# The prologue of an attention and MLP kernel: three query groups on the first keys, one token tile's statistics on ScalarE

## The chip, the cores and the metric

The kernel runs on one core of a Trainium2 chip. The core has five engines that run side by side, each with its own in-order queue: TensorE (PE, matrix products into PSUM; its weight loads are shown as PEld), VectorE (DVE), ScalarE (ACT), GpSimd (POOL) and SyncE (SP), which here only issues transfers between the main memory and the on-chip buffer SBUF. The metric is the time of one execution on the device, in microseconds. The kernel before takes 1042.89 us, the median of three runs from 1042.58 to 1043.29.

## The reference

```python
def _A_ref(x, wqkv, wo):            # S = 2048 tokens, D = 1024, H = 32 heads of 32
    qkv = (x @ wqkv).reshape(B, S, 3, H, Dh).transpose(2, 0, 3, 1, 4)
    q, k, v = qkv[0], qkv[1], qkv[2]
    p = softmax(einsum("bhqd,bhkd->bhqk", q, k) * Dh ** -0.5)
    o = einsum("bhqk,bhkd->bhqd", p, v)
    return o.transpose(0, 2, 1, 3).reshape(B, S, D) @ wo

def _B_ref(x, w1, b1, w2, b2):      # F = 3584
    h = gelu(layernorm(x) @ w1 + b1)     # tanh form
    return h @ w2 + b2

xn = layernorm(x)
out = x + _A_ref(xn, wqkv, wo) * silu(_B_ref(xn, w1, b1, w2, b2))
```

Everything is in bfloat16. The softmax takes no maximum off: the kernel raises the scaled scores directly.

## The kernel before, in words

**Tiles.** The 2048 tokens are 16 tiles of 128, and 8 blocks of 256. The 32 heads are 8 groups of 4 heads; a head group `hg` fills 128 rows. A *query group* is 256 queries of one head group, so there are 64 of them. A *unit* (`unit`, from L800) is one query group against one block of 256 keys: eight matmuls of scores into four PSUM banks (L811), two exponentials of 128x1024 on ScalarE (L820), which write a buffer of probabilities `P`, and later eight matmuls of the probabilities with the values. 512 units make 1024 exponentials. Six of the eight PSUM banks hold scores, so TensorE can be one and a half units ahead of ScalarE. The other two banks serve all other products, one item of work in each.

**Denominators.** For most query groups VectorE adds the probabilities pairwise into one tile (`tree`: four pair adds and three adds per query group) and TensorE sums this tile with a matrix of ones. In the first query groups, TensorE sums every unit's probabilities directly (`plain`). `quotient` divides.

**The prologue.** Ten token tiles are loaded at once into what later is the MLP's hidden buffer `hT` (`load_x`, L616); tiles 10 to 15 follow as buffers come free. Each tile gets two `bn_stats` of 512 columns and one `bn_aggr` on VectorE (L761, L763), an addition of epsilon (L767), a power of -0.5 on GpSimd (L769), and a normalization on VectorE (`normalize`, L738). Tiles 0 and 1 are groups of their own here, the others go in pairs. Tiles 0 to 3 are transposed by TensorE (`tr_item`, L725) and copied out of PSUM by ScalarE (L728); tiles 4 to 15 are transposed by a DMA that SP issues (L742). The result is `xnT`. For every block of 256 tokens, `k_item` computes the keys of head group 0 (copied to SBUF by ScalarE, L714), `q_item` or `qk_item` the queries (copied by VectorE, L704 and L694), and `v_item` the values (L682). While the keys come, only two query groups of head group 0 use them: the list `order0` (L1088) is (0,0), (0,1), (1,0), (1,1), and then for each further block (0,kp), (1,kp), each pair being a query group and a key block.

**Buffers.** There are ten buffers for probabilities, used in turn. The first 16 units also use six more that lie in the weight rings `w1r` and `w2r` of the MLP, which are not loaded until these have been read.

**After the prologue.** The units of the remaining query groups follow one another through all head groups. Between them TensorE does the projections of the next head group, the MLP (whose tanh also runs on ScalarE, L1004 and L1033), and at the end the output projection.

**The order of the work.** All queues are written by a planner (`_Plan`) before the kernel is built. Every operation has an assumed duration, a latency, a priority and the operations that it depends on, found by tokens such as `("xnT", t)` that it reads and writes. The planner plays the engines against the clock with these assumptions: at each moment an engine takes the ready operation of lowest priority number (`pick`). `plan.dense` holds the queues of TensorE's items, each item with a position, and some with a unit by which it is due. Scores go first as soon as their PSUM banks are free. Where TensorE has nothing to do, the planner puts in filler matmuls (L660). On the chip the order is then fixed, and only semaphores hold an engine up.

## Time and profile before

| what | us |
|---|---|
| median of three runs (lowest, highest) | 1042.89 (1042.58, 1043.29) |
| span of the profiled execution | 1042.1 |
| ScalarE busy | 1017.7 (98%) |
| TensorE busy, its weight loads | 1008.8 (97%), 640.8 (61%) |
| VectorE busy | 958.4 (92%) |
| first tile's statistics start on VectorE | 3.61 |
| first copy of a transposed tile on ScalarE | 8.79 |
| first exponential | 13.63 |
| key copies of blocks 0 to 7 on ScalarE | 12.74, 18.54, 25.09, 29.61, 34.23, 40.45, 44.07, 47.95 |
| last exponential ends | 1031.5 |

The profile is one execution; of that execution only the span from the first to the last instruction is known, and the runs' times, taken around the whole execution, are 0.5 to 1.2 us longer. In the lines that follow, a line of a timeline has the start, the length, the engine, the source line, the operation with output and input, and how many were merged; in brackets stands the idle time before it and what ended it. Lengths of merged rows overlap by a little, so the step from one instruction to the next is better taken from their starts. A line of waits has the waiting engine and line, what it waited for, the total, the number and the longest.

### The profile page before, as it was taken

What the parts mean: (1) busy time and instruction counts of PE and PEld (TensorE: products, weight loads), DVE (VectorE), ACT (ScalarE), POOL (GpSimd) and SP (SyncE); (2) the same over time, 40 slices, a digit from 0 to 9 for tenths busy, and PEclk for the clock granted to TensorE, in tenths of its full rate; (3) what the DMA queues carried; (4) which work ended last, traced back from release to release, by engine and by line L of the source; (5) the groups of instructions that cost most, each with busy time, mean ns of one, the idle gap of its engine ahead of it and who ended that gap; (6) DMA issues with size and microseconds to landing.
All of it is one profiled execution on the core that took longest, in us unless ns stands there. A gap on an engine that the chain in (4) does not pass through costs nothing.

```text
span 1042.1 us, 31753 instructions
## 1 busy us (share of the span) xinstructions
PE 1008.8 (97%) x14179; PEld 640.8 (61%) x14179; DVE 958.4 (92%) x1450; ACT 1017.7 (98%) x1129; POOL 11.0 (1%) x20
## 2 busy tenths in 40 slices
PE   9999899999999999999999999999999999999996
PEld 7555567666665676667665765666657655754442
DVE  8589998999899999998999989999999999878887
ACT  5899999999999999999999999999999999999996
POOL 1200000000000000000000000000000000000000
PEclk9999999999999999999999999999999999999999
DMA  8985558537654577376555674575456753763321
GB/s 198 193 224 145 128 169 226 143 98 204 183 167 127 152 210 217 91 185 181 149 143 157 175 219 128 125 198 169 135 137 195 204 168 121 224 212 111 105 82 52
DMA packets 318200, 168.00 MB, mean 161 GB/s; under 512 B 56688, under 2 KB 306032, under 8 KB 318064
## 3 DMA queue, kind: packets, MB, share of 16 engines
q1 hardware_dynamic: 318064, 165.98, 58.3%
q8 instruction: 111, 1.82, 0.7%
q14 instruction: 25, 0.20, 0.1%
HBM read 146.55 MB, written 12.06 MB: 152 GB/s over the span
## 4 chain that ended last, share of the span: by engine, by line
ACT 89%; PE 4%; DVE 3%; DMA 3%; SPq 0%; issue 0%; POOL 0%
ACT P L820 82%; ACT ut L1004 5%; PE ps L610 3%; ACT gw L1033 2%; DVE stats L761 1%; PE ps L605 1%; PE ps L811 1%; DMA hT<-in_A_x_dram 1%; DMA w2r<-in_B_w_dram 1%; ACT w1r L820 1%; DMA yst<-in_A_x_dram 1%; ACT w2r L820 1%; DMA xnT<-gw 0%; DVE gw L738 0%; DMA yT<-yst 0%
## 5 line engine op out<-in xcount | busy, mean ns | idle before, releaser
L820 ACT ACTIVATE P<-ps 128x1024 bf16<-128x1024 f32 x1012 | 956.6, 1237 | 4.3 <-PE ps L811 4.2
L837 DVE TENSOR_TENSOR PA<-P 128x2048 bf16<-128x2048 bf16 x178 | 216.4, 1219 | 26.3 <-ACT P L820 25.6
L610 PE MATMUL ps<-yT,w1r 128*128 128x256 bf16 x1792 | 227.5, 273 | 1.0 <-DVE xb L992 0.4
L610 PE MATMUL ps<-w2r,hT 128*128 128x256 bf16 x1792 | 222.3, 273 | 0.4 <-DMA w2r<-in_B_w_dram 0.4
L811 PE MATMUL ps<-QKT 32*128 32x256 bf16 x4096 | 203.3, 273 | 18.4 <-ACT P L820 16.7
L854 DVE TENSOR_TENSOR PR<-PR,PA 128x2048 bf16<-128x2048 bf16 x178 | 216.2, 1214 | 1.3
L610 PEld LDWEIGHTS ps<-yT,w1r 128*128 128x128 bf16 x1792 | 163.8, 98 | 51.7 <-issue 27.9
L610 PEld LDWEIGHTS ps<-w2r,hT 128*128 128x128 bf16 x1792 | 163.9, 98 | 48.1 <-issue 29.1
L811 PEld LDWEIGHTS ps<-QKT 32*128 32x128 bf16 x4096 | 60.7, 92 | 152.8 <-ACT P L820 146.6
L605 PE MATMUL ps<-P,V 128*32 128x256 bf16 x4048 | 138.0, 274 | 0.0
L610 PE MATMUL ps<-xnT,wqk 128*128 128x512 bf16 (+1 forms) x552 | 130.4, 365 | 0.2 <-ACT xnT L728 0.2
L605 PEld LDWEIGHTS ps<-P,V 128*32 128x32 bf16 x4048 | 96.1, 96 | 30.6 <-issue 22.8
L610 PE MATMUL ps<-wv,xnT 128*128 128x256 bf16 (+1 forms) x576 | 87.2, 285 | 2.7 <-DVE V L682 1.4
L610 PEld LDWEIGHTS ps<-xnT,wqk 128*128 128x128 bf16 x552 | 48.4, 98 | 51.2 <-issue 13.7
L992 DVE TENSOR_TENSOR xb<-ps,b1T 128x512 bf16<-128x512 f32 x112 | 76.6, 684 | 1.4 <-PE ps L610 1.0
L837 DVE TENSOR_TENSOR PR<-P 128x2048 bf16<-128x2048 bf16 x62 | 75.4, 1215 | 1.4 <-ACT P L820 1.1
L1004 ACT ACTIVATE ut<-ut 128x1024 bf16<-128x1024 bf16 x56 | 70.9, 1266 | 0.0
L610 PEld LDWEIGHTS ps<-wv,xnT 128*128 128x128 bf16 x576 | 52.1, 98 | 27.4 <-issue 11.2
L694 DVE CAST QKT<-ps 128x512 bf16<-128x512 f32 x59 | 40.4, 685 | 2.8 <-PE ps L610 2.4
L1001 DVE TENSOR_TENSOR ut<-xb 128x1024 bf16<-128x1024 bf16 x56 | 38.3, 683 | 0.2
L1003 DVE TENSOR_TENSOR ut<-ut,xb 128x1024 bf16<-128x1024 bf16 x56 | 38.0, 679 | 0.0
L909 DVE STREAM_TRANSPOSE nt<-ps 128x256 f32<-128x256 f32 x64 | 28.4, 443 | 10.3 <-PE ps L605 10.2
(76 smaller groups left out, 564.9 us busy)
## 6 DMA issues: line engine op xcount, KB each, us to landing
w1r<-in_B_w_dram SPq DMA_DIRECT2D x112, 512.0 KB, 4.5
w2r<-in_B_w_dram SPq DMA_DIRECT2D x128, 448.0 KB, 4.4
hT<-in_A_x_dram SPq DMA_DIRECT2D x20, 256.0 KB, 4.0
wqk<-in_A_wqkv_dram SPq DMA_DIRECT2D x16, 256.0 KB, 3.8
yst<-in_A_x_dram SPq DMA_DIRECT2D x16, 256.0 KB, 4.6
g_scratch<-gw SPq DMA_DIRECT2D x32, 128.0 KB, 3.9
o_scratch<-ot SPq DMA_DIRECT2D x56, 64.0 KB, 3.6
xnT<-o_scratch SPq DMA_DIRECT2D x7, 512.0 KB, 5.7
```

What stands on the lines that cost most here:

```text
L605: ins = e.matmul(dst(j), lhsT=lhsT(j), rhs=rhs(j), start=start, stop=stop, tile_position=(0, 32 * j), skip_group_check=True)
L610: return e.matmul(dst, lhsT=lhsT, rhs=rhs, start=start, stop=stop, skip_group_check=True)
L694: dve(lambda e: e.tensor_copy(QKT[sl][:, which, tq * 512:(tq + 1) * 512], bank(it.bank)), c_ps(512), [], [(nm, sl, 2 * tq), (nm, sl, 2 * t ...
L811: ins = e.matmul(bank(b0[j], kk * 256, (kk + 1) * 256), lhsT=QKT[sl][32 * j:32 * j + 32, 1, kb * 128:(kb + 1) * 128], rhs=QKT[sl][32 * j:3 ...
L820: x = act(lambda e, h=h: e.activation(Pt[pi][:, 2 * h:2 * h + 2].rearrange("p j k q -> p (j k q)"), ps[:, pr[h] * 1024:(pr[h] + 1) * 1024] ...
L837: return dve(lambda e: e.tensor_tensor(dst[:].rearrange("p u j q -> p (u j) q"), src[:].rearrange("p u j k q -> p (u j) k q")[:, :, 0, :], ...
L854: return dve(lambda e: e.tensor_tensor(fl3(pr), fl3(pr), fl3(PA[i]), op=ALU.add), c_b16(2048), [("PA", i), tok], [tok], 3.2)
L909: dve(lambda e: e.transpose(nt_t[:], bank(pv.bank, 256, 512)), c_ps(256) + 120, [], [("nt",)], prio, pv)
L992: dve(lambda e: e.tensor_tensor(xb_t[ui][:, half].rearrange("p (k t) -> p k t", k=2), bank(it.bank).rearrange("p (k t) -> p k t", k=2), b1 ...
L1001: dve(lambda e: e.tensor_tensor(u_, fl(xb_t[ui]), fl(xb_t[ui]), op=ALU.mult), c_b16(1024), xs, [("ut", ui)], 3)
L1003: dve(lambda e: e.tensor_tensor(u_, u_, fl(xb_t[ui]), op=ALU.mult), c_b16(1024), [("ut", ui)] + xs, [("ut", ui)], 3)
L1004: act(lambda e: e.activation(u_, u_, ACT.Tanh, scale=GC), c_acts(1024), [("ut", ui)], [("ut", ui)], 1)
```

## The change

Five things change, all of them in how the first 60 us are arranged; the computation is the same.

1. Three query groups instead of two (`NG0 = 3`) take part while the keys come. `order0` puts the units (2,0) and (2,1) behind block 2, (2,2) behind block 5, (2,3) behind block 6, and (2,4) to (2,7) behind the last of the first two groups. The queries of block 2 and block 3 become `q_item`s of 256 columns. The first four units of group 2 get buffers of their own (16 to 19): in the values' third slot, in the next head group's queries and in two pieces of the hidden buffer. Group 2 gets its denominators from TensorE.
2. Tile 1 (`AT = 1`) gets its mean and its mean of squares from two activations on ScalarE with an accumulator, and three small operations on VectorE turn them into the variance.
3. Tile 1's copy out of PSUM is made in two halves, and `xnT` is tracked by column block, so that a product can begin with the first half.
4. Tiles 2 and 3 become groups of their own; their loads go ahead of the first weights; the wait of tile 2's statistics for tile 1's normalization goes.
5. In the planner, VectorE's aggregates and epsilon additions go ahead of statistics, and in the first 16 us VectorE is held for up to 0.13 or 0.22 us when a more urgent operation is about to become ready.

```diff
+            if e == "DVE" and best is not None and 1 <= best.prio <= 1.2 and t < 16000.0:
+                for r, _, o in soon[e]:
+                    if r < t + (220.0 if o.prio > 0.96 else 130.0) and o.prio < best.prio - 0.04 and not o.dead:
+                        wake(r, e)
+                        return None
...
-        NTR, NWARM = 4, 8
+        NTR, NWARM, NG0, AT = 4, 8, 3, 1
...
+        Pt.append(V[:, 2].rearrange("p t n -> p (t n)").rearrange("p (j k q) -> p j k q", j=4, k=2))
+        Pt.append(QKT[1][:, 0].rearrange("p (j k q) -> p j k q", j=4, k=2))
         h_flat = hT[:].rearrange("p a b c -> p (a b c)")
+        for i in range(2):
+            Pt.append(h_flat[:, (3 + i) * 2048:(4 + i) * 2048].rearrange("p (j k q) -> p j k q", j=4, k=2))
...
-        load_x(0)
-        load_x(1)
+        for t in range(NTR):
+            load_x(t)
         wk0 = load_qk(0, 1)
         wq0 = load_qk(0, 0)
-        load_x(2)
-        load_x(3)
...
-            act(lambda e: e.activation(xnT[:, :, t * 128:(t + 1) * 128],
-                                       bankb(it.bank).rearrange("p (c t) -> p c t", c=DC), ACT.Copy),
-                c_act(1024), [tk], [("xnT", t)], 0, it)
+            for lo, hi in ((0, 4), (4, 8)) if t == 1 else ((0, 8),):
+                act(lambda e, lo=lo, hi=hi: e.activation(xnT[:, lo:hi, t * 128:(t + 1) * 128],
+                                                         bankb(it.bank)[:, lo * 128:hi * 128].rearrange("p (c t) -> p c t", t=128),
+                                                         ACT.Copy),
+                    c_act((hi - lo) * 128), [tk], [("xnT", t, c) for c in range(lo, hi)], 0, it)
...
-            groups = [(2 * n,), (2 * n + 1,)] if n == 0 else [(2 * n, 2 * n + 1)]
+            groups = [(2 * n,), (2 * n + 1,)] if n < 2 else [(2 * n, 2 * n + 1)]
             for ts in groups:
+                if ts == (AT,):
+                    for k, f, sc in ((0, ACT.Copy, 1.0 / D), (1, ACT.Square, D ** -0.5)):
+                        act(lambda e, k=k, f=f, sc=sc: e.activation(
+                            fl3(PA[0])[:, k * 1024:(k + 1) * 1024], xst[AT], f, scale=sc, accum_out=mv[:, AT, k:k + 1]),
+                            c_acts(1024) + 93, [XS(AT)], [("st", AT, k)], 1)
+                    dve(lambda e: e.tensor_tensor(lnp[:, AT:AT + 1, 2], mv[:, AT:AT + 1, 0], mv[:, AT:AT + 1, 0], op=ALU.mult), 65,
+                        [("st", AT, 0)], [("s2",)], 0.95)
+                    dve(lambda e: e.scalar_tensor_tensor(lnp[:, AT:AT + 1, 0], mv[:, AT:AT + 1, 1], EPS, lnp[:, AT:AT + 1, 2], op0=ALU.add,
+                                                         op1=ALU.subtract), 65,
+                        [("st", AT, 1), ("s2",)], [("ve", AT)], 0.95)
+                    dve(lambda e: e.tensor_tensor(mv[:, AT:AT + 1, 1], mv[:, AT:AT + 1, 1], lnp[:, AT:AT + 1, 2], op=ALU.subtract), 65,
+                        [("st", AT, 1), ("s2",)], [("mv", AT)], 1.1)
...
-                            605, [XS(t)], [("st", t, c)], 1.2, extra=[first[1]] if t == 2 else [])
+                            605, [XS(t)], [("st", t, c)], 1.2)
...
-                pro_q.append(q_item(n))
+            if n < NG0:
+                pro_q.append(q_item(n))
...
-                q0_q.append(qk_item(0, 0, n // 2, wq0, (0.5, 14.0, 28.0)[n // 2 - 1]))
-                q0_q[-1].due = 16 * (n // 2)
+                if n == 3:
+                    q0_q.append(q_item(3, "q0", 6.0))
+                else:
+                    q0_q.append(qk_item(0, 0, n // 2, wq0, (0.5, 14.0, 28.0)[n // 2 - 1]))
+                q0_q[-1].due = 16 * (n // 2) + (8 if n == 3 else 0)
...
-        pvs = [_Item("pv"), _Item("pv")]
-        us = [[], []]
-        order0 = [(0, 0), (0, 1), (1, 0), (1, 1)] + [(qb, kp) for kp in range(2, NKP) for qb in range(2)]
+        pvs = [_Item("pv") for _ in range(NG0)]
+        order0 = [(0, 0), (0, 1), (1, 0), (1, 1), (0, 2), (1, 2), (2, 0), (2, 1)]
+        for kp in range(3, NKP):
+            order0 += [(0, kp), (1, kp)]
+            if kp in (5, 6):
+                order0.append((2, kp - 3))
...
-        for qb in range(2):
+        for qb in range(NG0):
+            if qb == 2:
+                for kp in range(4, NKP):
+                    got[(2, kp)] = unit(0, 2, kp, pvs[2])
...
-                if w == 0 and qb < 2:
+                if w == 0 and qb < NG0:
```

More of the change, by code (lines that the diff above doesn't have):

```diff
@@ L691, in fn @@
                     return mm(e, bank(b), wqk[wi][:, dc, :], xnT[:, dc, tq * 512:(tq + 1) * 512], dc == 0, dc == DC - 1)
[L692 removed]
+                chunk(it, fn, Q512, [("xnT", 4 * tq + k, dc) for k in range(4)] + [("wqk", wi)])
             nm = "Q" if which == 0 else "K"
@@ L1103, in bass_recurrent_scan__mha_block__mixer_channel_mlp__prompt_kernel @@
             store_o(qb)
+        after([("V", 2, n) for n in range(NPR)], [("P", 16, h) for h in range(2)])
+        after([("Q", 1, n) for n in range(NPR)], [("P", 17, h) for h in range(2)])
+        after([("h", k) for k in range(12, NH)], [("P", i, h) for i in (18, 19) for h in range(2)])
         for i in range(3):
```

50 lines of the change are left out of this document (30 added, 20 removed).

## The prediction

> **What bounds the kernel now.** I read three things in this order: the first part of the page with the chain that ended last, ScalarE's own timeline of the first 60 us, and the waits and idle work of TensorE.
>
> ```profile
> span 1042.1 us, 31753 instructions
> ## 1 busy us (share of the span) xinstructions
> PE 1008.8 (97%) x14179; PEld 640.8 (61%) x14179; DVE 958.4 (92%) x1450; ACT 1017.7 (98%) x1129; POOL 11.0 (1%) x20
> ```
>
> ScalarE is busy 98% of the span, and the chain that ended last gives it 89%, of which 82% is one line, the exponentials of the scores. Merged in the chain, 100 of them take 91.67 us, so the step from one to the next is 0.917 us; the 1237 ns mean of the groups overlaps and is not used. From 47 us to 1031.5 us ScalarE has no idle slice worth a number (0.26 us in all, between 600 and 700 us). So the end is the moment at which ScalarE becomes saturated, plus a fixed amount of work. Time can only come from its idle time in the prologue:
>
> ```profile
> 19.43 5.63 ACT L820 ACTIVATE P<-ps 128x1024 bf16<-128x1024 f32 x6 [0.51 <-PE ps L811]
> 25.09 0.38 ACT L714 ACTIVATE QKT<-ps 128x256 bf16<-128x256 f32 x1
> 25.97 3.77 ACT L820 ACTIVATE P<-ps 128x1024 bf16<-128x1024 f32 x4 [0.50 <-PE ps L811]
> 29.61 0.42 ACT L714 ACTIVATE QKT<-ps 128x256 bf16<-128x256 f32 x1
> 31.50 2.86 ACT L820 ACTIVATE P<-ps 128x1024 bf16<-128x1024 f32 x3 [1.48 <-PE ps L811]
> 34.23 0.40 ACT L714 ACTIVATE QKT<-ps 128x256 bf16<-128x256 f32 x1
> 34.49 2.89 ACT L820 ACTIVATE P<-ps 128x1024 bf16<-128x1024 f32 x3
> 38.40 1.94 ACT L820 ACTIVATE P<-ps 128x1024 bf16<-128x1024 f32 x2 [1.01 <-PE ps L811]
> 40.45 0.38 ACT L714 ACTIVATE QKT<-ps 128x256 bf16<-128x256 f32 x1
> 41.34 2.85 ACT L820 ACTIVATE w1r<-ps 128x1024 bf16<-128x1024 f32 x3 [0.50 <-PE ps L811]
> ```
>
> The reader is to see a rhythm. Each L714 copies one block of 256 keys out of PSUM; these come every 3.6 to 6.6 us, while two query groups make only four exponentials (3.67 us) of each. Why the keys come at that pace is in the timeline of VectorE, which has no gap between 8.4 and 22.8 us:
>
> ```profile
> 14.80 0.65 DVE L761 BATCH_NORM_STATS2 stats<-hT 128x6 f32<-128x512 bf16 x1
> 15.36 0.16 DVE L767 TENSOR_SCALAR lnp<-mv 128x2 f32<-128x2 f32 x1
> 15.42 1.28 DVE L761 BATCH_NORM_STATS2 stats<-hT 128x6 f32<-128x512 bf16 x2
> 16.61 0.99 DVE L738 TENSOR_SCALAR gw<-hT,mv,lnp 128x1024 bf16<-128x1024 bf16 x2
> ```
>
> Here L738 normalizes tiles 4 and 5, the source of key block 2, and three statistics of tiles 6 and 7 stand before it.
>
> **The change, part by part.** Between the start of block 2's exponentials (25.97) and 47.05 lie 21.1 us. ScalarE does 18 exponentials in them (16.5) and 4 key copies at 0.28 from the chain (1.1), so 3.4 us are idle; the waits marked in the rows make 3.0 of it.
>
> 1. A third query group. After it, block 2 brings eight exponentials (7.3 us) and blocks 3 to 7 bring four or six, by the new list of units. With the old arrival times of the keys, ScalarE would finish block 2's eight at 33.3, when block 3 has been there since 29.6; the four of block 3 with its copy end at 37.3, block 4's at 41.2, and block 5's scores were there by 41.3. So one after another the 3.4 us fill: gain 3.4.
>
> 2. Block 2 sooner. On VectorE, tile 1 leaves: two statistics at a step of 0.62 (three start-to-end in 1.87) are 1.24 and an aggregate is 0.11; the wait of 0.35 for tile 2's load at 8.40 goes, as that load moves up. In come three small operations for tile 1 instead of one and a second addition of epsilon for tiles 2 and 3, about 0.08 each by the steps of L767: 0.25. Net 1.45. The new order (aggregates and epsilon ahead of statistics, and a short hold of VectorE) would also take statistics out from ahead of L738: at most the three above, 1.87; the one at 14.80 (0.56) and some 0.2 of the last are what it can surely free, because L738 must in any case wait 0.7 for GpSimd's power, which covers one statistic. I take 1.45 + 0.75 = 2.2. Lower end 0.5, if the holds (up to 0.22 each, some four before tile 5) take 0.95 back; upper end 1.45 + 1.87 = 3.3. What is late next is the pair of transposing loads of tiles 4 and 5 on SP (3.76 us for both from 17.18), then block 2's matmuls at 23.91; they follow L738 and move with it.
>
> 3. ScalarE gets tile 1's copy and square of 1024 columns: nearest row, the 1024-column copy out of PSUM, 1.03 us each, so 2.06. Tile 1 has landed by 4.85 at the latest (its first half is then in work), so they end by 6.9, inside the 6.6 us that ScalarE idles before 8.79. If that cover failed, the first exponential would be up to 2.1 later; that costs nothing either while the first eight exponentials wait for block 2. After a first exponential at about 12.3, eight of them, tiles 2 and 3's copies (1.87) and a key copy end at 21.8, and block 2's scores are due at 23.8: 2.0 us of cover.
>
> 4. Tile 1's copy in two halves: one more instruction, 0.07 us (from 0.28 for 256 columns and 0.93 for 1024), and the first matmuls may start half a copy, 0.45, sooner. Both lie within the same cover, so 0. The first keys come perhaps 1.3 us sooner, which moves nothing that ends last.
>
> 5. Loads: tiles 2 and 3 (512 KB) pass the first weights on SP. Data flowed at 235 to 275 GB/s while weights came and at 340 to 400 otherwise, by the bandwidth in slices of 0.3 us; the same six transfers end at about 7 to 8 us. The first use of the weights is at about 9.3. Cost 0; if they were 2 us late, part 3's cover takes it. The stalled issue (1.54 us for one) passes from tile 2 to tile 4, used after 10 us.
>
> 6. Group 2 now adds its denominators on TensorE (eight steps of 0.22, before one: +1.5 us), and VectorE loses seven adds of 1.21 (8.5 us). More sharply, TensorE must do the later work in 5 us less:
>
> ```profile
> PE ps L811 <- ACT P L820: 11.5, 21, 1.2
> ```
>
> ```profile
> 0.00:20.00 20.00, 11.13 (x141) 10.47 (x141) 1.00 0.79 192
> ...
> sum 1042.00, PE 21.93 PEld 18.88; mean PE 1.69 PEld 1.45
> ```
>
> The first row is TensorE's idle time before scores between 100 and 900 us; the second view is the filler matmuls, 21.93 - 11.13 = 10.8 us after 20 us. Some 22 us are spare, against 6.5 needed: 0. Without that cover the whole gain would go.
>
> By matmul busy time (97%) TensorE has 33 us left in the whole span. [...]
>
> 7. New waits. The queues are in order: at 28.84 VectorE waited 0.94 for tile 12's load with tile 11's aggregate behind it until 30.04. Such a misplaced wait can now cost ScalarE directly. Its bounds are 0 and 2.5 (the two largest old gaps, 1.48 and 1.01, again); block 5 is the tightest, due at 39.1 where ScalarE asks for it at 39.4. I take 0.7.
>
> Sum: 3.4 + 2.2 - 0.7 = 4.9 us off. The profiled span is 1042.1, and the median 1042.89 is 0.8 more; span 1037.2, time 1038.0. With the ends, 3.4 + 0.5 - 2.5 = 1.4 and 3.4 + 3.3 = 6.7, so 1036.2 to 1041.5.
>
> **Rivals.** (a) Keys stay as late: block 2 does not move (holds and loads eat part 2) and in-order waits take half of part 1 or more: 0 to 2 us off, 1040.9 to 1042.9. For it: tiles 10 to 15 wait for loads issued behind transposes on SP (28.84), which nothing here changes. Against: two tasks less ahead on VectorE.
>
> (b) Slower: the probability buffers. Unit (2,6) writes the buffer of (1,0), which group 1's product must have read. Before, that product started at about 55.5 after the last values (cast at 53.98) and the buffer was asked for at 56.6. Now ScalarE asks at about 58.9: twelve exponentials and two key copies after 41.2 in part 1 make 36 exponentials at 52.8, less 2.2, plus 0.7, is 51.3; eight more and a key copy are 7.6. In the meantime TensorE has three score units more ahead (1.3 us) and a third group's product close behind, 8 x 0.44 = 3.5 us. A delay of the values to 57 us would only eat the gain; it turns the sign when group 1's product starts more than 4.9 us after the request, near 64 us. With 7 to 9 us of such stall, 1045 to 1047. Against: TensorE is 96% busy from 50 to 60 and 98% from 60 to 80, but key, value and score work go ahead of the rest.
>
> (c) More: block 2 comes 3.3 sooner, nothing waits, and the head start of the first keys counts too (another 1.3): 8 us off, 1034.9.
>
> (d) The square makes ScalarE change its table. The trace has one load, 1.28 us at 0.72, for exponential, tanh and copy; it shows no square. Two more loads would put the first exponential 2.6 later, 0.6 beyond the cover: 1038.6. [...]
>
> **How the numbers follow.** The forecast 0.66 (its range 1036.2 to 1041.5), (a) 0.12, (b) 0.11, (c) 0.06, (d) 0.05. The measurement cannot tell less than 0.2%, 2.1 us, from no change, so faster means under 1040.8: most of the forecast (0.62 of 0.66), (c) and (d), 0.73; same is (a) and the rest of the forecast, 0.16; slower is (b), 0.11. The range runs from 1034.7, which takes in (c), to 1042.5, which leaves out (b) and a little of (a).
>
> **What would show it.** Block 2's key copy at 22.9 instead of 25.09, with eight exponentials behind it; ScalarE's idle time between the first exponential of block 2 and saturation under 1 us instead of 3.4; no statistic of tile 1 on VectorE; the first exponential near 12.3 instead of 13.63; 36 exponentials done near 51.3 us instead of 56.7; one table load. Wrong would be: a gap on ScalarE after 55 us (b), a wait of ScalarE for scores at blocks 4 to 6 of more than 2 us (a), or less idle time before 100 us with gaps between 600 and 700, where it was already 0.26.

## The result and the profile after

| what | before | after |
|---|---|---|
| median of 18 runs, us (lowest, highest) | 1043.09 (1041.59, 1044.37) | 1040.23 (1039.0, 1042.81) |
| ratio (95% interval) | 1 | 0.9972 (0.9965 to 0.9979) |
| span of the profiled execution | 1042.1 | 1039.2 |
| first exponential | 13.63 | 13.31 |
| block 2's first exponential | 25.97 | 22.41 |
| 41st exponential | 60.01 | 56.45 |
| key copies of blocks 2 to 7 | 25.09, 29.61, 34.23, 40.45, 44.07, 47.95 | 21.46, 28.76, 34.12, 38.71, 45.93, 48.95 |

The change takes 2.9 us off (0.28%), in the runs as in the two profiled executions; the forecast was 4.9. The result shows the span of every run: a run's time is 1.8 us more than its own span, not 0.5 to 1.2 us as the comparison of one span with other runs' times had it. So both profiled executions are some 0.8 us longer than their medians, and their spans can be compared.

The first lines of the page after, and its chain of work that ended last:

```profile
span 1039.2 us, 31689 instructions
PE 999.7 (96%) x14117; PEld 639.2 (62%) x14179; DVE 950.5 (91%) x1444; ACT 1020.1 (98%) x1134; POOL 11.7 (1%) x21
ACT 92%; PE 3%; DVE 3%; DMA 1%; issue 0%; POOL 0%
```

ScalarE bounds the kernel as before, and a little more of the chain is its own. Its timeline after, from the first work to the exponentials of block 6 (L771 are tile 1's statistics, L739 the copies of transposed tiles, L724 the key copies, L856 the exponentials):

```profile
0.72 1.28 ACT L655 ACT_TABLE_LOAD   x1 [0.72 <-PEq L1351]
4.14 1.06 ACT L771 ACTIVATE PA<-hT 128x1024 bf16<-128x1024 bf16 x1 [1.92 <-DMA hT<-in_A_x_dram]
5.10 0.19 ACT L771 ACTIVATION_READ_ACCUMULATOR PA<-hT 128x1 f32 x1
...
7.36 1.02 ACT L739 ACTIVATE xnT<-ps 128x1024 bf16<-128x1024 bf16 x1 [1.03 <-PE ps L735]
...
12.39 1.02 ACT L739 ACTIVATE xnT<-ps 128x1024 bf16<-128x1024 bf16 x1 [0.34 <-PE ps L735]
13.31 1.93 ACT L856 ACTIVATE P<-ps 128x1024 bf16<-128x1024 f32 x2
...
22.41 3.77 ACT L856 ACTIVATE P<-ps 128x1024 bf16<-128x1024 f32 x4 [0.50 <-PE ps L847]
...
35.98 2.85 ACT L856 ACTIVATE P<-ps 128x1024 bf16<-128x1024 f32 x3 [1.47 <-PE ps L847]
...
43.20 1.94 ACT L856 ACTIVATE w1r<-ps 128x1024 bf16<-128x1024 f32 x2 [1.34 <-PE ps L847]
...
70.30 9.34 ACT L856 ACTIVATE P<-ps 128x1024 bf16<-128x1024 f32 x10 [0.77 <-PE ps L847]
```

Two things are to be seen. Block 2 comes 3.6 us sooner, block 4 at the same time, and block 6 at 45.93, 1.9 *later* than before. And ScalarE still waits for scores in the middle blocks, and once more at 70.

It helps to keep one account for all kernels here. Count the exponentials along ScalarE's timeline, 0.917 us apart within a row. From the ninth (block 2's first) to the 41st lie 32 steps and five key copies, 32 x 0.917 + 5 x 0.28 = 30.7 us; the rest of that stretch is idle time. Before: 60.01 - 25.97 - 30.7 = 3.3. After: 56.45 - 22.41 - 30.7 = 3.3. **In this account ScalarE's idle time has not been filled at all, and block 2's earlier start of 3.56 is the whole gain**, and 0.5 of it is lost later (0.78, nearly all at 70 us, against 0.26 in all of the rest before). That leaves 3.56 - 0.52 = 3.0 of the 2.9. An account says where the time lies, not what caused it: no_hold below has no idle time left and an old start of block 2, and reaches the 41st exponential just as soon.

VectorE's timeline shows where block 2's start comes from (L787 and L789 are the statistics, L750 the normalizations):

```profile
13.70 0.21 DVE L789 BATCH_NORM_AGGREGATE mv<-stats 128x2 f32<-128x12 f32 x1
...
14.02 0.69 DVE L787 BATCH_NORM_STATS2 stats<-hT 128x6 f32<-128x512 bf16 x1
14.94 1.00 DVE L750 TENSOR_SCALAR gw<-hT,mv,lnp 128x1024 bf16<-128x1024 bf16 x2 [0.23 <-POOL lnp L796]
```

One statistic stands before the normalization of tiles 4 and 5 now, where three did. It starts at 14.94 instead of 16.61, 1.67 sooner. The pair of transposing loads then takes 2.68 us to issue instead of 3.76 (15.51 against 17.18, in SP's timeline), 1.08 sooner. The remaining 0.8 lies between these loads and the key copy.

TensorE's timeline shows why the middle blocks did not follow:

```profile
34.57 1.03 PE L619 MATMUL ps<-wv,xnT 128*128 128x256 bf16 x8 [0.80 <-DMA xnT<-gw]
41.88 0.94 PE L619 MATMUL ps<-wv,xnT 128*128 128x256 bf16 x7 [1.50 <-DMA xnT<-gw]
...
68.67 0.28 PE L847 MATMUL ps<-QKT 32*128 32x256 bf16 x3
69.88 0.39 PE L847 MATMUL ps<-QKT 32*128 32x256 bf16 x5 [0.92 <-issue]
```

Value products stand in TensorE's queue ahead of scores that are ready, and wait there for the transposing load of a tile. The last four of these loads were issued from 35.36 to 43.36 (before: 37.03 to 43.34): the head start of 1.67 is still there at tile 12 and gone at tile 15. The two last lines are another matter: TensorE stops in the middle of a group of eight, for 0.92 us, with nothing to wait for.

What stands against the spare time of TensorE, first in its waits from 100 to 900 us and then in the windows of the filler matmuls:

```profile
PE ps L847 <- ACT P L856: 12.0, 24, 1.2
```

```profile
0.00:20.00 20.00, 7.29 (x83) 6.80 (x83) 1.00 0.76 214
...
sum 1000.00, PE 16.85 PEld 14.31; mean PE 4.21 PEld 3.58
```

After 20 us there are 16.85 - 7.29 = 9.6 us of fillers and 12.0 of idle time before scores, 21.6 in place of 22.3. TensorE's spare time is as large as before, so the third group's extra work there has cost no time that can be seen.

### The profile page after: what moved, and what is told of

Its sections match the earlier page's. It is cut to its first block, busy times and chain, and to the rows that moved or that the text cites. A ratio compares the mean times of both kernels' runs of the same rounds, so it can differ in the third digit from the quotient of the medians.

```text
span 1039.2 us, 31689 instructions
## 1 busy us (share of the span) xinstructions
PE 999.7 (96%) x14117; PEld 639.2 (62%) x14179; DVE 950.5 (91%) x1444; ACT 1020.1 (98%) x1134; POOL 11.7 (1%) x21
## 3 DMA queue, kind: packets, MB, share of 16 engines
q8 instruction: 111, 1.82, 0.7%
## 4 chain that ended last, share of the span: by engine, by line
ACT 92%; PE 3%; DVE 3%; DMA 1%; issue 0%; POOL 0%
ACT P L856 84%; ACT ut L1037 5%; ACT gw L1066 2%; PE ps L619 1%; DVE stats L787 1%; PE ps L614 1%; DMA xnT<-gw 1%; PE ps L847 1%; DVE gw L750 0%; ACT w1r L856 0%; DMA hT<-in_A_x_dram 0%; DVE hT L1292 0%; DVE V L692 0%; ACT hT L856 0%; DVE mv L789 0%
## 5 line engine op out<-in xcount | busy, mean ns | idle before, releaser
L856 ACT ACTIVATE P<-ps 128x1024 bf16<-128x1024 f32 x1004 | 948.8, 1228 | 3.6 <-PE ps L847 3.6
L873 DVE TENSOR_TENSOR PA<-P 128x2048 bf16<-128x2048 bf16 x175 | 212.7, 1218 | 26.7 <-ACT P L856 25.9
L887 DVE TENSOR_TENSOR PR<-PR,PA 128x2048 bf16<-128x2048 bf16 x175 | 212.4, 1214 | 1.3
L619 PE MATMUL ps<-xnT,wqk 128*128 128x512 bf16 (+1 forms) x513 | 119.6, 360 | 3.6 <-issue 1.8
```

Source lines behind the costliest of these rows:

```text
L619: return e.matmul(dst, lhsT=lhsT, rhs=rhs, start=start, stop=stop, skip_group_check=True)
L856: x = act(lambda e, h=h: e.activation(Pt[pi][:, 2 * h:2 * h + 2].rearrange("p j k q -> p (j k q)"), ps[:, pr[h] * 1024:(pr[h] + 1) * 1024] ...
L873: return dve(lambda e: e.tensor_tensor(dst[:].rearrange("p u j q -> p (u j) q"), src[:].rearrange("p u j k q -> p (u j) k q")[:, :, 0, :], ...
L887: return dve(lambda e: e.tensor_tensor(fl3(pr), fl3(pr), fl3(PA[i]), op=ALU.add), c_b16(2048), [("PA", i), tok], [tok], 3.2)
```

## The experiments

The theory after the result: the third group fills nothing, because in-order products that wait for transposing loads replace the idle time; the gain is block 2's start. (Two of the runs below, no_hold from 750 us and old_loads from 210 us, also have another seed for the planner's later choices; what is read from their first 200 us is not touched by that.) The rivals: the third group is what counts and the rest only moves waits about; or the end is set by something else, such as the stop at 70.

All runs in one table; "idle" is ScalarE's, from the ninth to the 41st exponential, and "lost later" its idle time from there (or from 60 us, if that is later) to 1000 us.

| kernel | ninth | 41st | idle | lost later | median, us | ratio to before (95%) |
|---|---|---|---|---|---|---|
| before | 25.97 | 60.01 | 3.3 | 0.3 | | 1 |
| after | 22.41 | 56.45 | 3.3 | 0.8 | 1040.23 | 0.9972 (0.9965, 0.9979) |
| two_groups | 23.65 | 65.11 | 10.8 | 1.5 | 1049.82 | 1.0055 (1.0043, 1.0067) |
| third_only | 26.13 | 61.07 | 4.2 | 1.4 | 1052.62 | 1.0079 (1.0066, 1.0092) |
| third_only_again | 26.19 | 59.34 | 2.5 | 1.7 | 1045.3 | 1.0021 (1.0011, 1.0031) |
| late_transposes | 24.27 | 55.35 | 0.4 | 2.5 | 1040.66 | 0.9974 (0.9965, 0.9983) |
| two_late_transposes | 24.00 | 60.87 | 6.2 | 1.0 | 1046.3 | 1.0028 (1.0019, 1.0038) |
| late_loads | 22.90 | 55.78 | 2.2 | 5.5 | 1044.08 | 1.0004 (0.9992, 1.0016) |
| w2_later | 22.56 | 56.77 | 3.5 | 0.0 | 1040.47 | 0.9968 (0.9956, 0.9981) |
| late_from_10 | 23.22 | 56.42 | 2.5 | 0.1 | 1040.47 | 0.9970 (0.9959, 0.9982) |
| stats_on_vector | 25.38 | 57.55 | 1.5 | 0.3 | 1043.3 | 1.0005 (0.9995, 1.0014) |
| no_hold | 25.62 | 56.31 | 0.0 | 1.4 | 1041.37 | 0.9980 (0.9972, 0.9989) |
| old_loads | 25.84 | 61.30 | 4.8 | 1.8 | 1047.62 | 1.0046 (1.0032, 1.0059) |
| late_and_w2 | 24.79 | 56.10 | 0.6 | 0.7 | 1040.63 | 0.9975 (0.9966, 0.9984) |

The kernels ran in three groups, each on one chip beside the kernel before, whose medians were 1043.4, 1043.71 and 1043.24. The columns from the trace are of one execution each. How far two executions of the same order can differ is seen in third_only and third_only_again, whose orders part only at 540 us: their 41st exponentials lie 1.7 us apart. A smaller difference in that column is not read as an effect.

**The third group taken out of the changed kernel**

```diff
-        NTR, NWARM, NG0, AT = 4, 8, 3, 1
+        NTR, NWARM, NG0, AT = 4, 8, 2, 1
...
-        order0 = [(0, 0), (0, 1), (1, 0), (1, 1), (0, 2), (1, 2), (2, 0), (2, 1)]
-        for kp in range(3, NKP):
-            order0 += [(0, kp), (1, kp)]
-            if kp in (5, 6):
-                order0.append((2, kp - 3))
+        order0 = [(0, 0), (0, 1), (1, 0), (1, 1)] + [(qb, kp) for kp in range(2, NKP) for qb in range(2)]
```

> The changed kernel with two query groups instead of three while the keys come; everything else of the change stays. Theory: the third group is what turns the earlier block 2 into time, because with two groups ScalarE has only 3.67 us of work per key block and saturation still waits for the last keys, whose copies in the changed kernel came at 45.9 and 49.0 us against 44.1 and 48.0 before; so this kernel takes 1042 to 1043.5 us, no more than 1 us under the kernel before. Rival (the gain is VectorE's lighter start alone, the third group is idle filling): about 1040, like the changed kernel.

Measured 1049.82 us, slower than *before* by 5.7 by the ratio: a miss for theory and rival alike. ScalarE's largest wait is 3.25 us, at 43.61. TensorE's timeline has what it waited for, and a later stop:

```profile
42.41 0.61 PE L619 MATMUL ps<-wv,xnT 128*128 128x256 bf16 x2 [2.95 <-DMA xnT<-gw]
63.90 0.40 PE L614 MATMUL ps<-w2r,V 128*32 128x256 bf16 x7 [1.52 <-issue]
```

It is the same wait as after's at 41.88, twice as long, and with two groups there are fewer exponentials to stand in for it. So the third group does not leave the idle time as it was; it keeps it from growing to 10.8 us. The theory as I had it fell here.

**The third group alone, on the kernel before** (its statistics, loads, halves, priorities and no hold)

```diff
-        NTR, NWARM = 4, 8
+        NTR, NWARM, NG0, AT = 4, 8, 3, -1
...
-        order0 = [(0, 0), (0, 1), (1, 0), (1, 1)] + [(qb, kp) for kp in range(2, NKP) for qb in range(2)]
+        order0 = [(0, 0), (0, 1), (1, 0), (1, 1), (0, 2), (1, 2), (2, 0), (2, 1)]
```

> The kernel before with the third query group alone: tile 1 stays on VectorE, one copy per tile, the old order of loads, no hold and no new priorities on VectorE. The prediction's first part says 3.4 us off by itself (1039.7). Theory: about half of it is lost, because on TensorE value products of tiles whose transpose is still under way stand ahead of scores that are ready: 1041 to 1042. Rival (third group worth nothing without the earlier block 2): 1043.

1052.62 us, a miss. Most of it has nothing to do with the prologue. ScalarE's timeline has it at the very end:

```profile
1041.76 1.57 ACT L1281 ACTIVATE PR<-ps 128x512 bf16<-128x512 f32 x3 [8.04 <-PE ps L614]
```

Before and after this wait is 3.1 us. The planner had put the last output products behind one another. To see what is left without that, the same kernel was run with another seed for the planner's choices from 540 us on:

> The same kernel as third_only up to 540 us; from there the planner's order of the dense work is drawn with another seed. third_only took 9.2 us more than before, but its 33rd exponential started only 1.1 us later (53.82 against 52.76); 8.8 us of it lie after 1000 us, where ScalarE waited 8.0 us instead of 3.1 for the last product. Theory: that tail is an accident of the order that the planner finds at the end and has nothing to do with the third group: here the wait is 3.1 again and the time 1044 to 1046 (before plus 1.0 at the 41st exponential plus a stall of 1.2 at 72 us). So the third group alone brings nothing. Rival (the third group costs time in the whole kernel, TensorE falling behind): the tail stays, 1050 or more.

1045.3 us: the tail's wait is 3.16 again and 7.3 us are gone by the medians, 6.0 by the ratios. What is left of the third group alone is a loss of 2.2 us by the ratio: its 41st exponential is where it was before (0.7 sooner, less than two executions differ by), and 1.7 us are lost later instead of 0.3. In its prologue block 3's keys came out of a product that waited for a transposing load:

```profile
28.19 0.72 PE L612 MATMUL ps<-xnT,wqk 128*128 128x256 bf16 x5 [1.39 <-DMA xnT<-gw]
```

**A longer time assumed for the transposing loads.** The planner takes a transposing load to land 3.2 us after its issue began, if no other load is in the way: 1.3 for the issue, 0.87 for 256 KB at the assumed rate, and a latency of 1.0. In the changed kernel's trace the twelve loads take 2.8 to 6.5 us from the start of the issue to the landing. With a latency of 2.5 (4.7 in all) the planner places value products later.

```diff
-                    [("xnb", t % 4)], [("xnT", t, c) for c in range(DC)], prio=0, rate=300.0, occ=1300, lat=1000)
+                    [("xnb", t % 4)], [("xnT", t, c) for c in range(DC)], prio=0, rate=300.0, occ=1300, lat=2500)
```

> The changed kernel, but the planner assumes 1.5 us more until a transposing load has landed (its latency 2500 instead of 1000 ns), which alters only the order of some 50 groups of instructions on TensorE in the prologue. Theory: the two large waits of ScalarE in the changed kernel (1.47 us before 35.98 and 1.34 us before 43.20) come from value products that wait on TensorE for transposes while scores stand behind them; with the order made for later transposes these waits shrink to under 1.2 us together, and the time falls by 1 to 2 us, to 1038 to 1039.2. Rival (the keys themselves are late, the order does not matter): same waits, 1040.

In the prologue this did what it should: idle 0.4 instead of 3.3, and the waits for transposing loads ahead of scores are gone. But block 2 begins 1.9 later, the 41st exponential is only 1.1 sooner, and 2.5 us are lost after 60 us (0.88 near 70, 0.57 from 500 to 600, 1.07 from 600 to 700), 1.7 more than in the changed kernel. The time is the same as after's. The same with two groups:

> The changed kernel with two query groups and with the planner's 1.5 us more for transposing loads: against late_transposes it differs by the third group alone, and in neither do value products wait for transposes. Theory: the worth of the third group is what ScalarE idles here after block 2: with block 2 at about 24.3 and the last keys at 49 to 50, the 41st exponential starts 3 to 5 us later than the 55.35 of late_transposes, 1043.5 to 1046. Rival (third group worth nothing): within 1 us of late_transposes.

1046.3 us, 5.6 slower than with three groups (1.0028 against 0.9974), and the 41st exponentials are 60.87 and 55.35, 5.5 apart as well. So between these two kernels, which differ by the third group and what the planner makes of it (one value product still waits 1.48 for a transposing load with two groups), it is worth 5.6 us; on the kernel before it is worth less than nothing. And two groups with block 2 as early as 24.00 have their 41st exponential no sooner than the kernel before. **The earlier block 2 earns nothing without the third group, and the third group nothing on the kernel before.** Whether it is the earlier block 2 that the third group lacked there, the runs on single parts answer below: it is not.

**Fewer loads beside the transposing ones.** The next head group's weights and the first loads for the MLP wait for the last tile's normalization.

```diff
-            wk = load_qk(hg, 1, [first[9]] if hg == 1 else ())
+            wk = load_qk(hg, 1, [first[15]] if hg == 1 else ())
...
-                    [("yst", t2)], rate=390.0, extra=[first[11]] if c == 0 else ())
+                    [("yst", t2)], rate=390.0, extra=[first[15]] if c == 0 else ())
```

> The changed kernel, but the loads of the next head group's key weights and of the first two tiles for the MLP wait for the normalization of tile 15 instead of tiles 9 and 11, so they stand behind all transposes on SP; TensorE's order is the same as in the changed kernel. If the slow transpose of tile 12 (issued at 35.36, landed at 41.84, 6.5 us against a median of 3.3) is slow because these 768 KB were issued at 33.5 to 35.2 just ahead of it, it lands 2 to 3 us sooner, the wait of 1.34 us before 43.20 goes, and the time falls by about 1 us. Rival: the transposes slow one another; same landing, same time.

The transposing load of tile 12 lands 2.3 us sooner, as expected (39.51 instead of 41.84; 4.3 us from its issue instead of 6.5), and the wait before 43.20 is gone, but another before 36.65 has grown to 2.09. The 41st exponential is 0.7 sooner, within what two executions differ by. Then 5.5 us are lost, and the time is that of before by the ratio; the twelve times lie from 1039.92 to 1047.22. TensorE's timeline at that place, and the window around it (its last three columns are the granted clock, the DMA share and GB/s):

```profile
63.79 0.80 PE L619 MATMUL ps<-yT,w1r 128*128 128x256 bf16 x3 [3.50 <-issue]
...
65.06 2.95 PE L619 MATMUL ps<-yT,w1r 128*128 128x256 bf16 x13
```

```profile
60.00:80.00 20.00, 16.50 (x259) 9.76 (x250) 10.31 (x20) 14.46 (x17) 0.00 (x0) 0.83 0.99 261
```

It is the stop "issue" again, of 3.50 us, and behind it 13 products take 2.95 us instead of 1.59 in the changed kernel. The granted clock is 0.83 over these 20 us: 0.50 from 62.40 to 69.22 and 1.00 outside. It fell 2.1 us after the last product had ended (60.29).

**The stop taken away.** In the changed kernel four w2 loads share the DMA engines with the stop at 69; here they wait for the fourth product of the MLP.

```diff
-            dma(f"w2{i}", lambda e: e.dma_start(w2r[:, i], src), 458752, [], [("w2", i)], lat=3100.0)
+            dma(f"w2{i}", lambda e: e.dma_start(w2r[:, i], src), 458752, [], [("w2", i)], lat=3100.0,
+                extra=[w1ev[3]] if nw2["n"] <= 4 else ())
```

> The changed kernel, but the first four loads of the second MLP weights (1.8 MB, issued at 60.6 to 67.1) wait for the fourth product of the MLP; TensorE's order is the same up to about 75 us. At 69.3 in the changed kernel TensorE stopped for 0.92 us between the third and the fourth of eight score matmuls, with nothing it could have waited for, while the DMA engines were at full load, and ScalarE lost 0.77. Theory: the stop is TensorE's instructions arriving late behind these loads; it goes, and the time falls by 0.5 to 0.8 (less than the noise of the times, so the wait decides). Rival: it is not the load; the stop stays.

In this execution the stop is gone, and with it all of ScalarE's idle time from 60 to 1000 us. By the ratio (0.9968 against 0.9972) no gain can be told from noise; the profiled span is 1038.7 against 1039.2. The same together with the longer assumed time, for tiles 10 to 15 alone and for all:

> An attempt at a faster version: the changed kernel with the planner's 1.5 us more only for the transposes of tiles 10 to 15, so that block 2 keeps its place (22.4) and only later value products move back, and with the second MLP weights later as in w2_later. Theory: idle time of ScalarE between the 9th and the 41st exponential falls from 3.3 to about 1, the 41st starts at 54.5 instead of 56.45, and the time is 1037.5 to 1039. Rival (what is gained early is lost to later stalls, as in late_transposes, which was 1.1 ahead at the 41st exponential and ended 0.8 behind): 1040.

> An attempt at a better kernel: the changed kernel with 2500 instead of 1000 ns assumed for a transposing load, and the first four loads of w2 waiting for the fourth product of the MLP. Theory: the two losses of the changed kernel, waits behind transposing loads and the stop of TensorE at 69 us, are both gone; the 41st exponential starts at 55.4 us, 1.1 us earlier than in the changed kernel, nothing is lost between 60 and 80 us, and the time is 1038.5 to 1039.5 us. Rival: what the prologue gains, the order of the later work, drawn anew, gives back in gaps after 100 us, as in the first kernel with that assumption (1.64 us there): 1040 to 1041 us.

Neither beats the changed kernel beyond the noise. late_from_10 has no stop. late_and_w2 has idle time on TensorE at that place, which the profile puts down to VectorE:

```profile
68.89 0.71 PE L619 MATMUL ps<-yT,w1r 128*128 128x256 bf16 x5 [1.02 <-DVE PR L873]
```

That attribution does not hold. The operation named is a pair addition of probabilities, which this product does not read, and of the two PSUM banks for such products one is still being read by VectorE after the product has begun:

```profile
68.99 0.44 DVE L942 STREAM_TRANSPOSE nt<-ps 128x256 f32<-128x256 f32 x1
```

So the product uses the other bank, whose last reader on VectorE ended at 65.95. Its weights had landed by 65.85. With nothing left to wait for, I take this idle time for the same stop; the last section has more on it. late_and_w2's prologue, planned like that of late_transposes, was 0.75 later in this execution, and the rival's time came out (1040 to 1041), though by this stop at 69 and not by gaps after 100 us.

**What brings block 2 forward, one part at a time.** Tile 1's statistics on VectorE again:

```diff
-        NTR, NWARM, NG0, AT = 4, 8, 3, 1
+        NTR, NWARM, NG0, AT = 4, 8, 3, -1
```

> The changed kernel with tile 1's statistics on VectorE again, all else as after. The changed kernel began block 2's exponentials at 22.41 us, 3.56 earlier than before, where the prediction had 2.2, of which 1.45 for this part. If this part is worth what the prediction says, the two statistics and the aggregate come back ahead of tiles 2 to 5 and block 2's exponentials begin at 22.4 + 1.35 = 23.8 us. Rival: VectorE was not what brought block 2 forward; then they begin at 22.4 to 22.9 us. For the time: blocks 3 to 5 wait for transposing loads anyway, so of the 1.4 us I expect half at the end, 1041.0 us, between 1040.2 (nothing) and 1041.6 (all).

Block 2's exponentials begin at 25.38, 3.0 later than after and more than theory said. The normalization on VectorE and the keys' product on TensorE in this kernel:

```profile
16.76 0.53 DVE L750 TENSOR_SCALAR gw<-hT,mv,lnp 128x1024 bf16<-128x1024 bf16 x1
```

```profile
23.42 1.14 PE L619 MATMUL ps<-xnT,wqk 128*128 128x256 bf16 x9 [1.32 <-DVE V L692]
```

The transposing loads are issued 1.8 later (17.32 against 15.51; theory had 1.35), and then the keys' product finds its PSUM bank held by values that VectorE has yet to cast, 1.32. By the ratios the time goes up by 3.4 us, to that of before. Its eleven times lie wide apart, from 1041.42 to 1046.26, and the profile is of the quickest: its 41st exponential is only 1.1 later than after's. What the other runs lose isn't seen.

The planner's hold of VectorE taken out:

```diff
-            if e == "DVE" and best is not None and 1 <= best.prio <= 1.2 and t < 16000.0:
-                for r, _, o in soon[e]:
-                    if r < t + (220.0 if o.prio > 0.96 else 130.0) and o.prio < best.prio - 0.04 and not o.dead:
-                        wake(r, e)
-                        return None
```

> The changed kernel without the short hold of VectorE in the planner; one seed of the planner from head group 3 on is another. The prediction gave the new order on VectorE 0.75 us and took the hold as part of it. By that, block 2's exponentials begin at 23.0 to 23.2 us instead of 22.41 and the time is 1040.5 to 1041 us. Rival: the hold costs as much as it frees, because VectorE stands idle up to 0.22 us each time; then they begin at 22.2 to 22.6 us and the time is that of the changed kernel, 1040.2 us.

Block 2 is 3.2 later (25.62), where theory had 0.6 to 0.8: without the hold the planner normalizes tiles 4 to 7 in one go, and SP issues their four transposing loads one behind the other, from 16.29 to 22.42. **And yet the 41st exponential is at 56.31, where after has it**, with no idle time in between, and the time is 0.8 us longer by the ratios (0.9980 against 0.9972, intervals that overlap), of which a stop "issue" of 1.44 at 69.6 accounts for 0.7. ScalarE's timeline of this kernel (L717 are the key copies, L849 the exponentials):

```profile
25.62 2.85 ACT L849 ACTIVATE P<-ps 128x1024 bf16<-128x1024 f32 x3 [0.51 <-PE ps L840]
28.35 0.41 ACT L717 ACTIVATE QKT<-ps 128x256 bf16<-128x256 f32 x1
...
41.18 3.79 ACT L849 ACTIVATE w1r<-ps 128x1024 bf16<-128x1024 f32 x4
...
56.31 2.05 ACT L849 ACTIVATE P<-ps 128x1024 bf16<-128x1024 f32 x2
```

This is the third group doing what part 1 of the prediction said: block 2 begins only 0.35 sooner than in the kernel before, and all 3.3 us of idle time are filled. It also shows what became of block 2's 3.2 us in the changed kernel: there the 27th exponential starts at 43.20, behind the wait of 1.34, and here at 43.02. By then the head start has been waited away. (Block 3's keys come at 28.35 here, 2.7 after block 2's first exponential and not 6.4 as in after, so this is not a test of block 2's start alone.)

The old order of loads:

```diff
-        for t in range(NTR):
-            load_x(t)
+        load_x(0)
+        load_x(1)
         wk0 = load_qk(0, 1)
         wq0 = load_qk(0, 0)
+        load_x(2)
+        load_x(3)
```

> The changed kernel with the old order of loads on SP: the first two weight loads ahead of tiles 2 and 3; one seed of the planner from 120 us on is another. The prediction gave the loads 0.35 us, the wait for tile 2 at 8.40 us, and put the rest of the gain on VectorE. If so, block 2's exponentials begin at 22.8 us. Rival: with tile 1's statistics gone from VectorE, tile 2 is needed earlier, at about 7 us, and the old order makes VectorE wait for tiles 2 and 3 for as long as it saved: then they begin at 23.8 to 24.2 us, and the change of the loads and that of the statistics only work together. For the time 1040.5 us by the first and 1041.2 us by the second.

1047.62 us, far worse than either side said, although block 2 (25.84) is hardly later than in the two kernels above. In the table the order of the loads divides the kernels with three groups: the eight with the new order reach the 41st exponential between 55.35 and 57.55, the three with the old one (this and both third_only) between 59.34 and 61.30, whenever their block 2 begins. VectorE idles 1.3 us in three pieces between 5.3 and 7.6 us, where it has no statistics of tile 2 to do yet, as the rival had it, and runs late from there; the last four transposing loads go from 43.03 to 49.26 instead of 35.36 to 43.36. ScalarE then waits for block 6's keys, and TensorE stops once more:

```profile
51.10 0.39 ACT L724 ACTIVATE QKT<-ps 128x256 bf16<-128x256 f32 x1 [2.84 <-PE ps L617]
```

```profile
49.15 1.05 PE L617 MATMUL ps<-wv,xnT 128*128 128x256 bf16 x8 [1.54 <-DMA xnT<-gw]
...
71.46 0.39 PE L612 MATMUL ps<-P,V 128*32 128x256 bf16 x6
73.54 0.29 PE L612 MATMUL ps<-P,V 128*32 128x256 bf16 x2 [1.70 <-issue]
```

Here the account closes: the 41st exponential is 4.85 later than after's and 1.05 more are lost later, 5.9; the profiled spans differ by 6.0.

VectorE's timeline shows one way in which a late load does not stay a small delay. Its queue holds casts of values between the statistics, and a cast waits for a product that waits for a transposing load, which waits for a normalization on VectorE:

```profile
35.09 0.69 DVE L692 CAST V<-ps 128x512 bf16<-128x512 f32 x1 [1.18 <-PE ps L617]
...
39.46 0.69 DVE L692 CAST V<-ps 128x512 bf16<-128x512 f32 x1 [1.23 <-PE ps L617]
```

In this kernel the two casts alone put 2.4 us in front of the last tiles' normalizations, which come 7.7 later than after's (42.51 against 34.80); the rest of it I don't place. The changed kernel has the same circle with 0.56 and 0.48.

## Why the prediction was right and where not

The direction, the mechanism's place and the range were right: ScalarE bounds the end, the gain comes out of its prologue, and 1040.2 lies between 1034.7 and 1042.5 and in the likeliest case's own range of 1036.2 to 1041.5. The size was 2.9 instead of 4.9, and the way to it was not the sum as written.

- **The sum, 3.4 + 2.2.** The step that did not come out is the addition. no_hold has part 1 nearly whole with almost none of part 2, the changed kernel has part 2 and 3.3 us of idle time, and both reach the 41st exponential at 56.3 to 56.5. With block 2 sooner ScalarE comes sooner to block 4, whose keys came no sooner (34.12 against 34.23), and to the scores behind the value product of tile 12, whose transposing load landed later (41.84 against 40.85), and there it waits, 1.47 and 1.34. Part 1 alone, 3.4, is near the 3.0 that the account shows. That 4.9, with part 2 counted in full, still had a range that takes in 1040.2 is in part luck.
- **Part 1, the third group, 3.4 off.** As a mechanism it is shown by no_hold. But the step took the keys' old arrival times as given while the work between them grew, and in the runs they moved: with three groups on the kernel before, block 5 came at 41.68 instead of 40.45 and block 7 at 49.08 instead of 47.95, and nothing was gained. Its worth is not one number: 5.6 us (late_transposes against two_late_transposes), 8.7 by the ratios of two_groups and after, and -2.2 on the kernel before.
- **Part 2, block 2 sooner, 2.2.** It came 3.56 sooner: 1.67 by VectorE (1.45 and 0.75 had been taken, so these were a little too much), 1.08 by a quicker pair of transposing loads and 0.8 behind them, which the step had not counted. The key copy was due at 22.9 and came at 21.46. But this time does not go into the end one for one: no_hold and late_transposes begin block 2 3.2 and 1.9 later and reach the 41st exponential no later. Parts 1 and 2 are not terms of a sum.
- **Part 3, tile 1's statistics on ScalarE, cost 0.** They took 2.2 us instead of 2.06, from 4.14 to 6.33, and ScalarE idled another 1.03 behind them: covered, as said. The first exponential came at 13.31 and not at 12.3, because tile 2's or 3's copy went ahead of it (12.39). Nothing ended later for that.
- **Part 4, the halves, 0.** No run tells.
- **Part 5, the loads, 0.** Wrong as a statement on its own: with the rest of the change in place, the old order costs 6.0 us by the profiled executions and 7.7 by the ratios, and no kernel with three groups and the old order gained anything. The 0.35 for tile 2's wait, counted in part 2, was the price in the kernel before; with tile 1 off VectorE tile 2 is needed sooner.
- **Part 6, TensorE's spare time.** Right: 21.6 us of fillers and idle time are left of 22.3.
- **Part 7, new waits, 0.7.** In kind right, mis-sized: after's waits for scores in the middle blocks are 0.33 (at 32.29), 1.47 and 1.34, 3.1 in all, above the bound of 2.5, and at 70 there is another 0.77 that the step did not have. The 3.1 can be booked here or as part 1 not filled; no_hold speaks for here. That the waits stand behind value products in TensorE's queue, and not behind VectorE's statistics, was not foreseen.
- **Rival (a)** had part of the truth: blocks 4, 6 and 7 came no sooner, and in-order waits took about as much as part 1. Block 2 moved, which it denied. **Rival (b)**: no wait for probability buffers is to be seen. **(c)** had the earlier block 2 (3.3) but not the waits. **(d)**: one table load, at 0.72; the square changes nothing.
- Of the signs named, block 2's key copy, the missing statistic and the single table load came; the idle time under 1 us did not (3.3), and 36 exponentials were done near 52.8, not 51.3. No wait at blocks 4 to 6 exceeded 2 us.

What stays open: why the last four transposing loads need 8.0 us to issue in the changed kernel and 6.3 before. Most of the difference is one issue of 4.01 us, that of tile 13. With three loads moved from ahead of it (late_loads) it took 2.28, but in late_transposes, where such loads stand just ahead of it as in after, 1.86. Open, too, is which of the parts besides the third group and the order of the loads are needed, and through what chain the order of the loads comes to 4.85 us at the 41st exponential.

## What to carry to other kernels

In a prologue where several in-order queues feed one another, the value of an early start and the value of more work to fill gaps are not added (here 3.4 and 2.2 us were, less 0.7, and 2.9 came): price each by what is late next once the other is in place, and follow the last arrival (here the transposing loads of tiles 12 to 15), not the first one that moves. An account of idle time says where time lies; only a run without the part says whether the part earned it. Where a planner writes the whole order, a small edit redraws the rest of it: one seed moved the time by 6.0 us by the ratios, more than the edit under study, so compare the account of the place in question and not the time alone. And an assumed landing time that is too short, 3.2 us where some loads took 6.5, puts waiting products in front of ready ones; a longer one removed those waits here, but the time stayed the same, because block 2 came later and more was lost after 60 us.

## What was not expected of the hardware

**TensorE stops at fixed places of its instruction stream, as if instructions came late.** In seven of the fourteen profiled kernels TensorE stops between 60 and 74 us for 0.65 to 3.50 us with nothing to wait for ("issue"), often in the middle of a group of eight: x7 then x1 in no_hold, x6 then x2 in old_loads, x3 then x5 in after. So it was not semaphores alone that held TensorE up here: the profile shows none behind after's 0.92 us. Counted in weight loads from the start, five of these stops stand behind exactly the 987th (after, third_only, third_only_again, no_hold, old_loads), although they begin between 68.2 and 71.8 us and fall in different products. The idle times of 1.10 in late_transposes and 1.02 in late_and_w2 stand behind the 987th as well. The profile puts both down to VectorE, but the product that follows uses neither the tile nor the bank of the operation named: in late_transposes, too, VectorE still reads the other bank (68.29 to 68.73) when the product begins at 68.41.

```profile
68.41 0.71 PE L619 MATMUL ps<-yT,w1r 128*128 128x256 bf16 x5 [1.10 <-DVE nv L955]
```

A smaller stop of 0.34 us in third_only_again stands behind the 859th, 128 before, and the one of two_groups behind the 732nd, 255 before; only that of late_loads, behind the 803rd, does not fit the spacing. The page's list of DMA queues has this line:

```profile
q8 instruction: 111, 1.82, 0.7%
```

1.82 MB in 111 packets are 16.4 KB each, and the kernel's 14179 weight loads and as many matmuls make 28358 / 111 = 255 instructions to a packet, the spacing of the stops (128 weight loads with their matmuls). So I take this queue for TensorE's, an estimate from these counts. The trace has the packets of the queue: all seven idle times behind the 987th weight load end 1.4 to 1.6 us after one of them has been transferred (in after it ended at 68.26, and TensorE went on at 69.88). That these stops are late instructions is what I read from these numbers; what makes them late is not shown. In w2_later, with four loads moved, the packet ended at 67.97 and TensorE passed the place at 69.32 without a stop. But late_and_w2 has the same four loads moved and stopped for 1.02, after 10 us at 222 GB/s. stats_on_vector passed without a stop after 10 us at 298 GB/s, and third_only stopped after 10 us at 209.

**An accumulator output cost a second instruction on ScalarE**: each of the two activations with one in the changed kernel is followed by a read of the accumulator, 0.19 us long (at 5.10 and at 6.14); from the first read to the next activation is a step of 0.10.

**Transposing loads vary by more than twice**: in the changed kernel's prologue 2.8 to 6.5 us from the start of the issue to the landing, and 1.24 to 4.01 us for one issue (before 1.23 to 2.38), for tiles of the same size.
